# Keys, queries and values laid out in DRAM in longer runs, and fourteen staging tiles for bias rows in place of six

## The chip, the cores and the metric

The kernel runs on one core of one Trainium2 chip, in one launch. The metric is device time in microseconds (us), the median of the runs; lower is better.

## The reference

Attention with a bias that a small network makes from positions, then two feed-forward stages. Cut to what matters:

```python
# q, k, v: (2, 8, 576, 64); w1: (1, 32), b1: (32,), w2: (32, 8)
scores = scale * np.matmul(q, k.transpose(0, 1, 3, 2))
psi_rel = np.log1p(np.abs(pos[:, None] - pos[None, :]))
x = (psi_rel / psi_i)[..., None]
h = np.maximum(x @ w1 + b1, 0.0)           # 576 x 576 x 32
bias = h @ w2                              # 576 x 576 x 8, the same for both batches
scores = scores + bias.transpose(2, 0, 1)[None]
attn = softmax(scores)                     # over the last axis
x = np.matmul(attn, v)                     # then as 1152 x 512 rows
x = (silu(x @ w_gate) * (x @ w_val)) @ w_out     # 512 -> 1536 -> 512
out = softplus(x @ w_in) @ w_out2                # 512 -> 2048 -> 512
```

## The kernel before, in words

The program has three stretches. First the bias of all heads is made and laid out in SBUF, then attention runs over eight units (a pair of heads, a batch), then the two feed-forward stages follow. This change touches the first stretch and the loads of the second.

**Bias rows.** The bias is made in 36 rows of work (`order`: numbers 32 to 35 first, then 0 to 31; a row is named here by its place in this order, from 0). For a row, `hidden` (line 246) makes four hidden tiles `r` of 128 x 576 from the table `G`, three on VectorE (L260) and one on ScalarE (L258); `second` (L264) multiplies them with `w2` in sixteen small matmul passes on TensorE into a PSUM tile `pb` of which there are two; `keep` (L277) scales `pb` on ScalarE into half of a staging tile in SBUF (`early`, L280). A DMA on the queue of SyncE (SP) then takes the 128 staged partitions apart into sixteen partitions of a bias tile, eight heads of 576 each (L284; for the first four rows two DMAs of four heads each, L287). A row's staged data is 128 x 576 x 4 bytes, 288 KB. The loop makes `r` two rows ahead; there are twelve buffers for `r`, three rows.

**Staging.** `staging` (L158) walks in a circle over six halves of three tiles, which are the tags `a4`, `a5`, `a6` of the pool `xp`; `a7` holds the queries of the second unit. The tags `a0` to `a3` belong from the start to the pairs `B11` and `T1` (L121), in which the attention output and a sum are kept for the feed-forward stage; their first writer is `finish` of the first unit (L453). A staging half is written again only when the DMA out of it has landed.

**Loads.** `load` (L161) fetches a pair of heads, transposed, as 64 partitions x 2 x 576; as the tile needs the data twice, in partitions 0 to 63 and in 64 to 127, it issues two DMAs of 288 KB each, in source runs of 2304 bytes. `load_v` (L177) fetches 384 KB of values in runs of 768 bytes and two small pieces (`vt`). Issued on SP before the bias rows, after the table: keys, queries and values of the first unit, keys and queries of the second.

**What sets the order.** In the first two stretches the instructions of PE, ACT, DVE, POOL and SP stand in the order in which they are written. All DMAs of SP go round over eight semaphores, so that one is issued only when the one eight before it has landed. `run_slot` (L498) is one step of attention: scores on TensorE (L304, for the first two units), the sum with the bias on VectorE (L352), the exponential on ScalarE (L366), transposes (L401) and products with the values (L428). Four of these steps (`EARLY`, rows 23, 26, 31 and 33) run among the bias rows; the others after them. Steps are counted from 0 too: steps 0 and 1 read `bias[0]`, 2 and 3 `bias[1]`, 4 to 7 the same tiles for the second unit, 8 and 9 `bias[2]`, 10 the mixed tile, and step 11 is the first to read `bias[3]`, whose last row is the 36th.

Of the kernel before, what the change touches and what calls it, by code (L numbers as in the profile page):

```python
# [11 lines left out]
F32 = mybir.dt.float32  # L12
# [7 lines left out]
P = 128  # L20
B, H, S, D, HID = 2, 8, 576, 64, 32
NP = H // 2
# [27 lines left out]
ROWS = np.r_[:256, 512:S, 256:512]  # L50
# [47 lines left out]


@with_exitstack  # L100
def tile_kernel(ctx: ExitStack, tc, qT, kT, vS, wb, wg, wv, wo, wi, wo2, table, out):
    nc = tc.nc
    sp = nc.sync
    const = ctx.enter_context(tc.tile_pool(name="const", bufs=1))
    xp = ctx.enter_context(tc.tile_pool(name="xp", bufs=1))
# [9 lines left out]
    def slots(pool, tag, names):  # L115

        for name in names:
            n = len([1 for t in SLOTS.values() if t[0] == tag])
            SLOTS[name] = (tag, [pool.tile([P, 2, S], F32R, tag=f"{tag}{2 * n + i}", name=f"{name}{t}") for i, t in enumerate("hl")])

    slots(xp, "a", ("B11", "T1"))  # L121

    def opener(stack):
        return lambda name, bufs, **k: stack.enter_context(
            tc.tile_pool(name=name, bufs=bufs, reuse_waits="tile", **k)
        )

    rctx = ExitStack()
    with ExitStack() as actx:
# [18 lines left out]
        def new_pairs(name, count, pool=pool, **k):  # L148

            ep = pool(name, 1, **k)  # L150
            for _ in range(count):
                pairs.append(ep.tile([P, 2 * S], F32, name=f"e{len(pairs)}"))
            return ep

        new_pairs("ep0", 2)
        qraw = pool("qraw", 1)
        early = [xp.tile([P, 2, S], F32, tag=f"a{i}", name=f"early{i}") for i in range(4, 8)]
        staging = itertools.cycle([t[:, i] for t in early[:3] for i in range(2)])  # L158
        psS = pool("psS", 2, space=PSUM)

        def load(r, src, pr, b):  # L161
            for d in range(2):
                sp.dma_start(
                    out=r[D * d : D * (d + 1)], in_=src[b, 2 * pr : 2 * pr + 2].rearrange("h d s -> d h s")
                )

        def load_k(i):
            pr, b = UNITS[i]
            kr = kp.tile([P, 2, S], F32, tag="kst", name="kr") if i < PLAIN else bias[0][:, :2]
            load(kr, kT, pr, b)  # L170
            return dict(i=i, pr=pr, b=b, kr=kr)

        def load_q(u):
            u["qr"] = early[3] if u["i"] == 1 else qraw.tile([P, 2, S], F32, tag="qr", name="qr")
            load(u["qr"], qT, u["pr"], u["b"])

        def load_v(u):  # L177
            pr, b = u["pr"], u["b"]
            v = u["v"] = vp.tile([P, 4, 3 * D], F32, name="v")
            vt = u["vt"] = vts[u["i"] % 3]  # L180
            sp.dma_start(out=v, in_=vS[b, pr, :512].rearrange("(c p) e -> p c e", p=P))
            thirds = lambda ap: ap.rearrange("p (t e) -> p t e", t=3)
            sp.dma_start(out=thirds(vt[:D])[:, ::2], in_=thirds(vS[b, pr, 512:])[:, ::2])
            sp.dma_start(out=vt[D:, D : 2 * D], in_=vS[b, pr, 512:, D : 2 * D])

        def high(h, src, by="a"):
            if by == "a":
# [58 lines left out]
        def hidden(i):  # L246
            s = order[i]
            c, t = divmod(s, 8)
            rs = []
            for ct in range(4):  # L250
                if c < 4:
                    w0 = cut + GU0 - (P * c + 32 * ct + t)
                else:
                    w0 = TU0 - (P * c + 16 * ct + t)
                r = rp.tile([P, S], F32, name="r")
                n = 4 * s + ct
                if ct == 3:
                    nc.scalar.activation(r, G[:, w0 : w0 + S], AF.Relu, bias=PB[:, n : n + 1])  # L258
                else:
                    nc.vector.tensor_scalar(r, G[:, w0 : w0 + S], PB[:, n : n + 1], 0.0, op0=ALU.add, op1=ALU.max)  # L260
                rs.append(r)
            return rs

        def second(rs):  # L264
            pb = psB.tile([P, 2, 512], F32, tag="B", name="pb")
            for hf in range(2):
                for ct in range(4):
                    nc.tensor.matmul(  # L268
                        pb[32 * ct : 32 * ct + 32, hf, :HALF],
                        W2,  # L270
                        rs[ct][:, HALF * hf : HALF * (hf + 1)],
                        start=True,
                        stop=True,
                    )
            return pb

        def keep(s, pb):  # L277
            c, t = divmod(s, 8)
            st = next(staging)
            nc.scalar.activation(  # L280
                st.rearrange("p (a n) -> p a n", a=2), pb[:, :, :HALF], AF.Copy, scale=inv[:, s : s + 1]
            )
            if c < 4:
                sp.dma_start(out=bias[c][t : t + 121 : 8], in_=st)  # L284
            else:
                for a in range(2):
                    sp.dma_start(out=bias[c][D * a + t : D * a + t + 61 : 4], in_=st[a::2])  # L287
# [197 lines left out]

        units, late = [load_k(0)], []
        load_q(units[0])
        load_v(units[0])
        units.append(load_k(1))
        load_q(units[1])  # L490
        chunks = [(i, sub, n) for i in range(2 * NP) for sub in range(2) for n in range(4 + sub)]
        chunks[4:13] = chunks[9:13] + chunks[4:9]
# [76 lines left out]
        with tc.manual_schedule(engines={E.PE, E.Activation, E.DVE, E.Pool, E.SP}):  # L569
            warm = psS.tile([P, 2, 512], F32, tag="S", name="warm")  # L570
            for _ in range(WARM):
                nc.tensor.matmul(warm[:, 0, :P], ident, ident, start=True, stop=True)

            nc.vector.tensor_scalar(PB, PB, wb_sb[:, 1:2], None, op0=ALU.mult)
            nc.vector.tensor_scalar(G[:, :TW], G[:, :TW], wb_sb[:, 0:1], None, op0=ALU.mult)
            hid = [hidden(i) for i in range(2)]
            for i, s in enumerate(order):
                pb = second(hid.pop(0))
                if i == 0:
                    nc.vector.tensor_scalar(G[:, cut:], G[:, cut:], wb_sb[:, 0:1], None, op0=ALU.mult)  # L580
                if i + 2 < len(order):
                    hid.append(hidden(i + 2))
                keep(s, pb)
                if i in EARLY:
                    run_slot()
            sctx.close()
            pool = opener(actx)
            ep1 = new_pairs("ep1", 4, opener(right), side="right")
            tmpp = pool("tmpp", 1)
            t2f = tmpp.tile([P, 2, S], F32, name="t2f")  # L590
            for i, mp in enumerate((tmpp, ep1)):
                mixes.append(mp.tile([P, 5 * P], F32, name=f"m{i}"))
                nc.gpsimd.memset(mixes[-1][:, S:], 0.0)
            atp = pool("atp", 6)
            fp = pool("fp", 1)
            psT = pool("psT", 3, space=PSUM)
            psO = pool("psO", 1, space=PSUM)
            while slot < len(chunks) or jobs or turned or gathered or done or late:
                run_slot()
# [36 lines left out]
    def as_float(n):  # L636


        x = cvp.tile([P, 2 * NK, P], F32, tag="x", name="x")
        load(2 * n + 3)  # L640
        for j in range(2):
            raw, y = loaded[2 * n + j], x[:, NK * j : NK * (j + 1)]
            hw, lw, yi = raw[:, :, :, 1], raw[:, :, :, 0], y.bitcast(I32)
            if n < NL2:
                nc.scalar.activation(y, hw.bitcast(F32), AF.Prelu, scale=2.0**-112, alpha=-(2.0**32))
            else:
                nc.scalar.activation(y, hw.bitcast(F32), AF.Copy, scale=2.0**-112)  # L647
            nc.vector.tensor_scalar(yi, yi, 3, None, op0=ALU.logical_shift_left)  # L648
            if n >= NL2:
                nc.vector.scalar_tensor_tensor(yi, hw, -(2**31), yi, op0=ALU.bitwise_and, op1=ALU.bitwise_or)  # L650
            nc.vector.scalar_tensor_tensor(yi, lw, 29, yi, op0=ALU.logical_shift_right, op1=ALU.bitwise_or)  # L651
            load(2 * n + j + 4)
        return x
# [340 lines left out]
    for k in range(2):  # L994
        t4 = row()
        h, l = [ap.bitcast(F32) for ap in X["T2"][k]]
# [50 lines left out]
    with tc.manual_schedule(engines={E.PE}):  # L1047
        quads = {"z": z}
        for q in range(4):
# [5 lines left out]
            for word in f"{OTHER if q else FIRST} {TAIL}".split():  # L1055
                who, what = word
                if who in "tu":
# [7 lines left out]
                    for i, t in enumerate(TOKENS[n]):  # L1065
                        if who == "t":
                            continue
                        a, ps = acc[t // 2][:, t % 2], held[n][:, i]
# [12 lines left out]
                getattr(quads[who], "p" + what)()  # L1081


_INS = ["qT", "kT", "vS", "wb", "wg", "wv", "wo", "wi", "wo2", "table"]


# [32 lines left out]
```

## Time and profile before

| | |
|---|---|
| median of 3 runs | 596.39 us (596.32 to 596.82) |
| the profiled execution | 596.96 us |
| its span, first to last instruction | 595.0 us |
| what lies around the span | 1.96 us |
| TensorE busy over the span | 578.5 us, 97% |
| the bias rows | 5.6 us (first `r`) to 63.8 us (last staged row) |
| instructions | 11346 |

The times of the stretches below are counted from the span's start. The views used are the page, the chain of waits (what was released last, in order of time), busy time by stretch, and the timelines of single engines, which give each group of instructions with the idle time ahead of it in brackets and who ended that.

### The profile page before, as it was taken

How to read it: one execution, taken by the hardware profiler on the slowest of the kernel's cores; microseconds unless marked ns; L12 is line 12 of the kernel's file. 1: busy time of each engine (PE TensorE's matmuls, PEld its weight loads, DVE VectorE, ACT ScalarE, POOL GpSimd, SP SyncE). 2: the span in 40 equal slices, each digit the busy share in tenths (PEclk: the TensorE clock that was granted, in tenths of full speed). 3: DMA queues.
4: the chain of work that ended last, by engine and by line, in shares of the span. 5: the costliest groups of instructions: out<-in, count | busy, mean ns of one | idle time of the engine just before them, and what ended most of it. 6: DMA issues, size and time to landing. Idle time of an engine off the chain costs nothing.

```text
span 595.0 us, 11346 instructions
## 1 busy us (share of the span) xinstructions
PE 578.5 (97%) x4274; PEld 506.3 (85%) x4274; DVE 454.2 (76%) x972; ACT 375.5 (63%) x711; POOL 98.8 (17%) x147
## 2 busy tenths in 40 slices
PE   8789999999999999999999999999999999999997
PEld 5233569888887999999999999999989989988986
DVE  6799687788888999897789735679998976983432
ACT  6699877778988876665558424349735734733520
POOL 0000477778993000000000000000000000000000
PEclk9899999999999999999999999999999999999999
DMA  9999924334442333324226222222444240310012
GB/s 216 223 204 210 192 80 108 97 88 111 110 128 82 121 96 110 101 79 135 72 89 194 72 72 72 74 83 64 135 138 136 81 142 8 136 35 1 2 54 105
DMA packets 47414, 63.30 MB, mean 106 GB/s; under 512 B 4480, under 2 KB 35200, under 8 KB 47360
## 3 DMA queue, kind: packets, MB, share of 16 engines
q1 hardware_dynamic: 47216, 62.57, 38.2%
q8 instruction: 33, 0.54, 0.4%
q14 instruction: 21, 0.17, 0.1%
q10 hardware_dynamic: 144, 0.02, 0.0%
HBM read 49.60 MB, written 2.36 MB: 87 GB/s over the span
## 4 chain that ended last, share of the span: by engine, by line
PE 83%; DMA 6%; DVE 5%; ACT 3%; issue 1%; POOL 1%; SPq 0%; ACTq 0%; DVEq 0%; POOLq 0%
PE pw L726 37%; PE pw L1034 17%; PE pw L677 13%; PE po L428 6%; PE ps L331 4%; DMA bias<-early 4%; PE pt L401 3%; DMA early<-in_qT_dram 1%; PE pb L268 1%; PE ps L304 1%; DMA qr<-in_qT_dram 1%; ACT early L280 1%; DVE e L352 1%; ACT e L366 1%; DVE bias L352 0%
## 5 line engine op out<-in xcount | busy, mean ns | idle before, releaser
L1034 PE MATMUL pw<-oh,g2h 128*128 128x512 f32 x144 | 56.2, 390 | 0.0
L1034 PE MATMUL pw<-oh,g2l 128*128 128x512 f32 x144 | 56.2, 390 | 0.0
L1034 PE MATMUL pw<-ol,g2h 128*128 128x512 f32 x144 | 56.1, 390 | 0.0
L268 PE MATMUL pb<-r,wb_sb 128*32 128x288 f32 x576 | 46.6, 426 | 7.8 <-ACT early L280 6.8
L260 DVE TENSOR_SCALAR r<-G 128x576 f32<-128x576 f32 x108 | 47.7, 516 | 4.3 <-PE pb L268 4.0
L268 PEld LDWEIGHTS pb<-r,wb_sb 128*32 128x32 f32 x576 | 18.8, 112 | 34.6 <-ACT early L280 18.9
L677 PE MATMUL pw<-gl,sh 128*128 128x384 f32 x144 | 48.2, 335 | 0.0
L677 PE MATMUL pw<-gh,sl 128*128 128x384 f32 x144 | 48.2, 334 | 0.0
L677 PE MATMUL pw<-gh,sh 128*128 128x384 f32 x144 | 48.2, 334 | 0.0
L651 DVE SCALAR_TENSOR_TENSOR x<-raw,x 128x512 int32<-128x512 int32 x68 | 46.3, 688 | 0.9
L374 POOL TENSOR_SCALAR e<-e,sm 128x576 f32<-128x576 f32 x44 | 34.4, 793 | 73.2 <-DVE sm L371 66.9
L352 DVE CUSTOM_DVE_ANT_0 e<-ps,bias 128x576 f32<-128x576 f32 x44 | 33.0, 750 | 13.2 <-PE ps L331 7.6
L408 ACT COPY at<-pt 128x512 f32<-128x512 f32 (+2 forms) x69 | 36.4, 547 | 6.4 <-PE pt L401 5.9
L331 PE MATMUL ps<-kst,ql 128*128 128x288 f32 x120 | 37.0, 337 | 2.0 <-DVE sm L352 1.4
L428 PE MATMUL po<-at,v 128*64 128x256 f32 (+3 forms) x384 | 36.8, 332 | 1.0 <-DVE at L408 0.8
L1072 DVE TENSOR_TENSOR acc<-pw,acc 128x512 f32<-128x512 f32 x27 | 17.5, 686 | 25.1 <-PE pw L1034 25.1
L366 ACT ACTIVATE e<-e,sm 128x576 f32<-128x576 f32 x44 | 34.3, 780 | 2.7 <-DVE sm L352 1.7
L648 DVE TENSOR_SCALAR x<-x 128x512 int32<-128x512 int32 x68 | 28.8, 428 | 9.3 <-ACT x L647 5.1
L428 PEld LDWEIGHTS po<-at,v 128*64 128x64 f32 x384 | 26.7, 137 | 8.2 <-issue 1.3
L331 PE MATMUL ps<-kst,qh 128*128 128x288 f32 x120 | 32.1, 295 | 0.0
L1034 PEld LDWEIGHTS pw<-oh,g2l 128*128 128x128 f32 x144 | 27.0, 188 | 5.8
L401 PE MATMUL pt<-ident,e 128*128 128x128 f32 x188 | 31.6, 276 | 0.1
(269 smaller groups left out, 1657.4 us busy)
## 6 DMA issues: line engine op xcount, KB each, us to landing
raw<-in_wo_dram SPq DMA_DIRECT2D x28, 512.0 KB, 3.5
bias<-early SPq DMA_DIRECT2D x32, 288.0 KB, 7.5
raw<-in_wi_dram SPq DMA_DIRECT2D x16, 512.0 KB, 3.8
raw<-in_wv_dram SPq DMA_DIRECT2D x12, 512.0 KB, 4.5
raw<-in_wg_dram SPq DMA_DIRECT2D x12, 512.0 KB, 3.5
qr<-in_qT_dram SPq DMA_DIRECT2D x14, 288.0 KB, 4.1
bias<-in_kT_dram SPq DMA_DIRECT2D x12, 288.0 KB, 4.6
v<-in_vS_dram SPq DMA_DIRECT2D x8, 384.0 KB, 3.6
```

Of the source, the lines that this page charges most:

```text
L260: nc.vector.tensor_scalar(r, G[:, w0 : w0 + S], PB[:, n : n + 1], 0.0, op0=ALU.add, op1=ALU.max)
L268: nc.tensor.matmul(pb[32 * ct : 32 * ct + 32, hf, :HALF], W2, rs[ct][:, HALF * hf : HALF * (hf + 1)], start=True, stop=True,)
L331: nc.tensor.matmul(ps[:, hf, :HALF], u[t][:, o : o + P], kst[:, a, HALF * hf : HALF * (hf + 1)], start=i == 0, stop=i == len(parts) - 1,)
L352: nc.vector.tensor_tensor_reduce(out=e[:, :S].rearrange("p (a n) -> p a n", a=2), in0=ps[:, :, :HALF], in1=bt.rearrange("p (a n) -> p a n" ...
L366: nc.scalar.activation(e, e, AF.Exp, bias=sm[:, 0, n : n + 1], scale=-1.0, accum_out=sm[:, 1, n : n + 1])
L401: nc.tensor.transpose(pt[:, P * w : P * (w + 1)], e, ident)
L408: marks[eng, u["i"], u["sub"]] = copy(at[:, :w], pt[:, :w]).ins
L428: nc.tensor.matmul(u["po"][D * a : D * (a + 1), o : o + n], v[:, D * t : D * (t + 1)], at[:, i : i + n], start=piece == 0 and o == 0, stop ...
L651: nc.vector.scalar_tensor_tensor(yi, lw, 29, yi, op0=ALU.logical_shift_right, op1=ALU.bitwise_or)
L677: nc.tensor.matmul(ps[:, :n], w[:, k], x, start=first and k == 0 and i == 0, stop=last and k == NK - 1 and i == 2)
L726: nc.tensor.matmul(ps[:, hf, :HALF], a[:, o + k], b[:, HALF * hf : HALF * (hf + 1)], start=start and k == 0 and i == 0, stop=k == 1 and i ...
L1034: nc.tensor.matmul(ps, g, w.rearrange("p k f -> p (k f)"), start=f == 0 and i == 0, stop=f == 3 and i == 2)
```

## The change

The host lays the inputs out anew: queries and keys as 128 partitions (the 64 rows twice) of 1152 elements, a run of 4608 bytes each, and the first 512 rows of the values as 128 partitions of 768 elements, a run of 3072 bytes. The last 64 rows of the values become an input of their own, `vT`. A load of keys or queries is then one DMA of 576 KB in place of two of 288 KB; the bytes are the same. The pairs `B11` and `T1` are taken from the pool only when the bias rows are done, and the tags `a0` to `a3` serve for staging until then: fourteen halves in place of six.

```diff
-    slots(xp, "a", ("B11", "T1"))
...
-        early = [xp.tile([P, 2, S], F32, tag=f"a{i}", name=f"early{i}") for i in range(4, 8)]
-        staging = itertools.cycle([t[:, i] for t in early[:3] for i in range(2)])
+        early = [xp.tile([P, 2, S], F32, tag=f"a{i}", name=f"early{i}") for i in range(8)]
+        staging = itertools.cycle([t[:, i] for t in early[:7] for i in range(2)])
...
         def load(r, src, pr, b):
-            for d in range(2):
-                sp.dma_start(
-                    out=r[D * d : D * (d + 1)], in_=src[b, 2 * pr : 2 * pr + 2].rearrange("h d s -> d h s")
-                )
+            sp.dma_start(out=r, in_=src[b, pr].rearrange("p (h s) -> p h s", h=2))
...
-            u["qr"] = early[3] if u["i"] == 1 else qraw.tile([P, 2, S], F32, tag="qr", name="qr")
+            u["qr"] = early[7] if u["i"] == 1 else qraw.tile([P, 2, S], F32, tag="qr", name="qr")
...
-            sp.dma_start(out=v, in_=vS[b, pr, :512].rearrange("(c p) e -> p c e", p=P))
+            sp.dma_start(out=v, in_=vS[b, pr].rearrange("p (c e) -> p c e", c=4))
...
             sctx.close()
+            slots(xp, "a", ("B11", "T1"))
...
+    def twice(a):
+
+        a = a.reshape(B, NP, 2, S, D).transpose(0, 1, 4, 2, 3).reshape(B, NP, D, 2 * S)
+        return np.concatenate([a, a], 2)
+
     given = {
...
+        "qT": twice(np.stack([q[:, h][:, ROWS if h % 2 else slice(None)] for h in range(H)], 1)),
+        "kT": twice(k),
+        "vS": vs[:, :, :512].reshape(B, NP, 4, P, 3 * D).transpose(0, 1, 3, 2, 4).reshape(B, NP, P, 12 * D),
+        "vT": vs[:, :, 512:],
```

No instruction of PE, ACT, DVE or POOL changes its place. On ACT the rows that stage a bias row (the one with `early` as its output) name other tiles, and wait for other DMAs (`DMAHW` with a number is one of the eight semaphores of the DMAs). Before, the seventh row and those after it:

```order
L280 ACTIVATE early_115<-pb,G 128x576 [waits PE_49]
L258 ACTIVATE r<-G 128x576 [waits Activation_49]
L280 ACTIVATE early_113<-pb,G 128x576 [waits DMAHW7_49,DMAHW6_49,PE_49]
L258 ACTIVATE r<-G 128x576 [waits Activation_49]
L280 ACTIVATE early_113<-pb,G 128x576 [waits DMAHW1_49,DMAHW0_49,PE_49]
```

And now, from the fourteenth row:

```order
L275 ACTIVATE early_115<-pb,G 128x576 [waits PE_49]
L253 ACTIVATE r<-G 128x576 [waits Activation_49]
L275 ACTIVATE early_109<-pb,G 128x576 [waits DMAHW3_49,DMAHW2_49,PE_49]
L253 ACTIVATE r<-G 128x576 [waits Activation_49]
L275 ACTIVATE early_109<-pb,G 128x576 [waits DMAHW5_49,DMAHW4_49,PE_49]
```

The wait of row n for the DMA of row n - 6 has become one for the DMA of row n - 14. On SP the head of the queue before:

```order
L243 DMA G<-in_table_dram 128x1064
L163 DMA kr<-in_kT_dram 64x2x576 x2
L163 DMA qr<-in_qT_dram 64x2x576 x2
L181 DMA v<-in_vS_dram 128x4x192
L183 DMA vt_96<-in_vS_dram 64x2x64
L184 DMA vt_96<-in_vS_dram 64x64
L163 DMA kr<-in_kT_dram 64x2x576 x2
L163 DMA early_116<-in_qT_dram 64x2x576 x2
L287 DMA bias_89<-early_113 16x4x576 x4
```

And now:

```order
L238 DMA G<-in_table_dram 128x1064
L160 DMA kr<-in_kT_dram 128x1152
L160 DMA qr<-in_qT_dram 128x1152
L176 DMA v<-in_vS_dram 128x768
L178 DMA vt_92<-in_vT_dram 64x2x64
L179 DMA vt_92<-in_vT_dram 64x64
L160 DMA kr<-in_kT_dram 128x1152
L160 DMA early_116<-in_qT_dram 128x1152
L282 DMA bias_85<-early_109 16x4x576 x4
```

The eight DMAs of halves have become four of 128 partitions each; the order of what is loaded is the same. On ACT the first writers of `B11` and `T1` (L453 and L480) now wait for the DMAs of the rows that were last staged in those tiles, the 29th and 30th and the 33rd and 34th.

## Rows read from the trace of the kernel before

**Rows 1.** The page: busy time of the engines; DMA share in 40 slices.

```profile
PE 578.5 (97%) x4274; PEld 506.3 (85%) x4274; DVE 454.2 (76%) x972; ACT 375.5 (63%) x711; POOL 98.8 (17%) x147
DMA  9999924334442333324226222222444240310012
```

**Rows 2.** Stretches: length, busy us (instructions) of each engine, granted clock, DMA share, GB/s.

```profile
0.00:20.00 20.00, 16.30 (x152) 9.85 (x152) 15.20 (x36) 11.38 (x16) 1.29 (x9) 1.00 0.94 223
20.00:44.00 24.00, 19.49 (x252) 7.39 (x256) 19.71 (x46) 21.66 (x32) 0.00 (x0) 0.93 1.04 208
44.00:64.00 20.00, 18.88 (x228) 7.93 (x220) 17.44 (x45) 19.28 (x33) 2.27 (x3) 1.00 1.04 211
...
22.00:24.00 2.00, 1.94 (x20) 0.98 (x24) 0.00 (x0) 1.96 (x4) 0.00 (x0) 0.57 1.03 213
```

**Rows 3.** The chain that ended last: start us, us, what; DMAs from issue to landing.

```profile
10.54 8.62 DMA early<-in_qT_dram
19.17 6.79 DMA bias<-early
...
30.72 7.63 DMA bias<-early
...
41.98 7.76 DMA bias<-early
...
71.51 2.31 PE po L428 x20
```

**Rows 4.** ScalarE's timeline: start us, us, instruction, [idle before, who ended it].

```profile
11.49 0.74 ACT L280 ACTIVATE early<-pb,G 128x576 f32<-128x576 f32 x1 [0.56 <-PE pb L268]
...
15.37 0.74 ACT L280 ACTIVATE early<-pb,G 128x576 f32<-128x576 f32 x1
...
21.26 0.74 ACT L280 ACTIVATE early<-pb,G 128x576 f32<-128x576 f32 x1 [4.49 <-DMA bias<-early]
...
50.47 0.77 ACT L366 ACTIVATE e<-e,sm 128x576 f32<-128x576 f32 x1
...
63.07 0.74 ACT L280 ACTIVATE early<-pb,G 128x576 f32<-128x576 f32 x1 [0.32 <-PE pb L268]
```

**Rows 5.** VectorE's timeline, with the same columns.

```profile
8.83 11.67 DVE L260 TENSOR_SCALAR r<-G 128x576 f32<-128x576 f32 x27
24.03 1.38 DVE L260 TENSOR_SCALAR r<-G 128x576 f32<-128x576 f32 x3 [3.53 <-PE pb L268]
...
45.38 0.76 DVE L352 CUSTOM_DVE_ANT_0 e<-ps,bias 128x576 f32<-128x576 f32 x1 [0.80 <-PE ps L304]
...
51.36 0.15 DVE L370 TENSOR_SCALAR sm<-sm 128x1 f32<-128x1 f32 x1 [0.67 <-ACT e L366]
...
59.14 2.66 DVE L260 TENSOR_SCALAR r<-G 128x576 f32<-128x576 f32 x6
...
63.78 0.76 DVE L352 CUSTOM_DVE_ANT_0 e<-ps,bias 128x576 f32<-128x576 f32 x1 [1.02 <-PE ps L304]
...
74.56 0.76 DVE L352 CUSTOM_DVE_ANT_0 e<-ps,bias 128x576 f32<-128x576 f32 x1 [2.51 <-PE ps L304]
```

**Rows 6.** TensorE's timeline: one bias row.

```profile
33.50 1.18 PE L268 MATMUL pb<-r,wb_sb 128*32 128x288 f32 x16 [0.28 <-ACT early L280]
```

**Rows 7.** L284, its last DMA (duration ns, first to last issue us; landing).

```profile
L284 SPq DMA_DIRECT2D bias<-early x1: 532/532/532, 63.8 to 63.8; - x1
...
DMA to landing us min/median/max: 6.9/6.9/6.9
```

**Rows 8.** L163, the first half of the second unit's keys.

```profile
L163 SPq DMA_DIRECT2D kr<-in_kT_dram x1: 595/595/595, 7.1 to 7.1; - x1
...
DMA to landing us min/median/max: 8.0/8.0/8.0
```

**Rows 9.** L628, the first three weight loads, 512 KB over 128 partitions each.

```profile
L628 SPq DMA_DIRECT2D raw<-in_wv_dram x2: 373/440/507, 173.0 to 174.0; - x2
...
DMA to landing us min/median/max: 3.7/4.7/5.6
```

More of the change, by code (lines that the diff above doesn't have):

```diff
@@ L100, in tile_kernel @@
 @with_exitstack
-def tile_kernel(ctx: ExitStack, tc, qT, kT, vS, wb, wg, wv, wo, wi, wo2, table, out):
+def tile_kernel(ctx: ExitStack, tc, qT, kT, vS, vT, wb, wg, wv, wo, wi, wo2, table, out):
     nc = tc.nc
@@ L180, in load_v @@
             vt = u["vt"] = vts[u["i"] % 3]
-            sp.dma_start(out=v, in_=vS[b, pr, :512].rearrange("(c p) e -> p c e", p=P))
+            sp.dma_start(out=v, in_=vS[b, pr].rearrange("p (c e) -> p c e", c=4))
             thirds = lambda ap: ap.rearrange("p (t e) -> p t e", t=3)
-            sp.dma_start(out=thirds(vt[:D])[:, ::2], in_=thirds(vS[b, pr, 512:])[:, ::2])
-            sp.dma_start(out=vt[D:, D : 2 * D], in_=vS[b, pr, 512:, D : 2 * D])
+            sp.dma_start(out=thirds(vt[:D])[:, ::2], in_=thirds(vT[b, pr])[:, ::2])
+            sp.dma_start(out=vt[D:, D : 2 * D], in_=vT[b, pr, :, D : 2 * D])
         def high(h, src, by="a"):
@@ L1081, in tile_kernel @@
                 getattr(quads[who], "p" + what)()
-_INS = ["qT", "kT", "vS", "wb", "wg", "wv", "wo", "wi", "wo2", "table"]
+_INS = ["qT", "kT", "vS", "vT", "wb", "wg", "wv", "wo", "wi", "wo2", "table"]
 def kernel(q, k, v, w1, b1, w2, moe_w_gate, moe_w_val, moe_w_out, moe2_w_in, moe2_w_out):
@@ L1095 @@
         small[rows, 0], small[rows, 1], small[rows, 2 + 8 * g : 10 + 8 * g] = w1[0], b1, w2
+    vs = np.concatenate([v[:, ::2], np.roll(v[:, 1::2], -D, 2), v[:, 1::2]], 3)
+    def twice(a):
+        a = a.reshape(B, NP, 2, S, D).transpose(0, 1, 4, 2, 3).reshape(B, NP, D, 2 * S)
+        return np.concatenate([a, a], 2)
     given = {
-        "qT": np.stack([q[:, h][:, ROWS if h % 2 else slice(None)] for h in range(H)], 1).transpose(0, 1, 3, 2),
-        "kT": k.transpose(0, 1, 3, 2),
-        "vS": np.concatenate([v[:, ::2], np.roll(v[:, 1::2], -D, 2), v[:, 1::2]], 3),
+        "qT": twice(np.stack([q[:, h][:, ROWS if h % 2 else slice(None)] for h in range(H)], 1)),
+        "kT": twice(k),
+        "vS": vs[:, :, :512].reshape(B, NP, 4, P, 3 * D).transpose(0, 1, 3, 2, 4).reshape(B, NP, P, 12 * D),
+        "vT": vs[:, :, 512:],
         "wb": small,
```

## The prediction

> **What bounds the kernel now.** I read the page first. TensorE is busy for 97% of the span, so time can only be won where it waits, and the DMA engines are at 9 tenths or more in the first five slices alone, some 74 us [rows 1]. The table by stretch narrows this: from 20 to 64 us the DMA share is 1.04, no engine of the sixteen is ever empty, at about 210 GB/s, while DVE is busy for 37.2 of these 44 us and ACT for 40.9 [rows 2]. The chain of waits says who holds whom: from 10.5 to 50 us it goes from DMA to DMA, each 7 to 9 us from issue to landing, with short ScalarE steps between [rows 3]. ScalarE's timeline has the place: unstalled it stages a row each 1.29 us (11.49 to 15.37 is three rows), then it waits 4.49 us for the first bias DMA to give a staging half back [rows 4]. From there on the row's pace is the DMA's: the issues at 30.72 and 41.98 stand eight rows apart, 1.41 us a row [rows 3]. [...]
>
> **How late the DMA may be.** After the rows the work is attention's own. The last bias DMA is issued at 63.84 and lands 6.9 us later, at 70.7 [rows 7]; its first reader, step 11, starts at 74.56 on VectorE and had waited for TensorE [rows 5], which was at products until 73.8 [rows 3]. So the bias data is 3.8 us ahead of its need at the end, though it holds the rows back at the start. What counts for the end is when step 4 can start: 63.78 now, after the last `r` ends at 59.14 + 2.66 = 61.8 and TensorE's last rows behind it [rows 5].
>
> **Fourteen staging halves.** The wait for the DMA of row n - 6 becomes one for row n - 14. In its new place row 14 (counted from 0) is staged by ScalarE at 11.49 + 12 x 1.29 = 27 us and needs row 0, whose two DMAs landed before 21.3 when staging went on [rows 4]; the backlog grows by 1.41 - 1.29 = 0.12 us a row, 2.5 us by row 35, so the wait does not come back. Who is late next:
> VectorE. From 8.83 it makes 27 tiles in 11.67 us, 0.432 us each [rows 5]. Up to the end of the last `r` it has 102 of them, 44.1 us; three sums of the early steps at 0.76, 2.3; and two small operations, 0.3. That ends at 8.83 + 46.7 = 55.5, where it now ends at 61.8: a gain of 6.3. Two waits in this stretch are not for a DMA: 0.80 for scores and 0.67 for an exponential [rows 5]. If both stay, the gain is 4.8. Most of them should go, since they arise while VectorE runs up to two rows ahead of a held ScalarE; at its own pace it arrives later. I keep a third, 0.5: 5.8.
> ScalarE. Rows 2 to 35 at 1.29, and three exponentials at 0.77: the last row would be staged at 11.49 + 42.7 + 2.3 = 56.5 against 63.07 [rows 4], a gain of 6.6: close, but VectorE is the bound.
> TensorE. A row takes 1.18 us [rows 6] and gives 0.11 us of room against 1.29; its idle stretch and the low clock behind it go too.
> So step 4 starts 5.8 us sooner, at 58.0, and step 11 at 68.8 if the bias is there.
>
> **The loads.** Eight halves and the values stand in the queue ahead of the rows. The first half of the second keys lands at 7.1 + 8.0 = 15.1 [rows 8] and the last half of the queries, three later, at 10.54 + 8.62 = 19.2 [rows 3]: 1.35 us for 288 KB. Weight loads over 128 partitions land two in (174.0 + 5.6) - (173.0 + 3.7) = 2.9 us, 1.45 us for 512 KB [rows 9], so 576 KB cost 1.63 in place of 2.70. Four of these pairs: 4.3 us. The values, 384 KB in one DMA over 128 partitions before and after, I cost at no gain; were they as slow as a half now, and as fast as the weights then, it would be 1.80 - 1.09 = 0.7 us. So the bias DMAs, which queue behind, start 4.3 us sooner and keep their 1.41 (the queue was full and stays full), and the last row lands at 70.7 - 4.3 = 66.4, 2.4 us before step 11 wants it. Bounds of this term: 0 (loads as slow as now) to 5.0. Its worth for the end by itself is nothing; it keeps the last row off the path, which at 70.7 would hold step 11 up by 1.9. The later loads, two DMAs fewer a unit on SP, lie under TensorE's work: the chain from 71 us on is compute [rows 3], and I cost them at nothing. The second unit's values and the third unit's keys queue behind the last bias row in the same order as now, and land 4.3 us sooner or, if loads gain nothing, when they do now.
>
> [...]
>
> **B11 and T1.** Their first writers on ScalarE now wait for rows staged late. T1 waits for the 34th of the 36, which is to land two rows ahead of the last, at 66.4 - 2.8 = 63.6; B11 for the 30th, about 57.9. `finish` of the first unit comes after the products that end at 73.8 now [rows 3], so at 68.0: B11's wait is 10 us over by then, and T1 comes later still. Queued behind it on ScalarE would be copies for the products; I cost it at nothing.
>
> **The rivals.**
> 1. The loads stay as slow as they are, and the last row ends the matter. The run lengths are what the change names, and the weights' loads speak against run length as the cause: theirs are of 1024 bytes, shorter than the 2304 now, and are faster. Then only the joining of halves could help, and if it doesn't, the last row lands at 70.7, step 11 starts there and not at 74.56: a gain of 3.8, 592.6. [...]
> 2. The three engines don't reach their own pace together: the two waits stay, and the other three early steps too cost VectorE the 0.8 that the first does now. The gain is 4.8 - 2.4 = 2.4, 594.0. For it: the coupling is tight, two PSUM tiles, three rows of `r`. Against: only the first sum shows such a wait.
> 3. Eight DMAs in flight slow each other. In rows: 36 rows take 70.7 - 19.2 = 51.5 us now, 1.43 each. From 19.2 - 4.3 = 14.9 they would take the last past 68.8 at a pace over 1.50, and so eat into the gain; at 1.66 step 11 is no sooner than now, and at 1.70, a fifth slower, the last lands at 76.1, 1.5 past 74.56: 597.9, slower than before. Against it: the share is 1.04 already, so each engine has always had a next packet; for it, only that six in flight is all the trace shows.
> 4. The gain is real and is lost again, in attention or at the start of the feed-forward stage: 596.4. The chain has no DMA after 50 us that is not a wait of compute, so I find no place for it.
>
> **How the numbers follow.** The profiled execution has a span of 595.0 and a time of 596.96; 5.8 off makes 589.2 and 591.2. Against the median, 0.57 lower, it is 596.39 - 5.8 = 590.6. Chances: the forecast (gain 4.8 to 6.6) 0.70; rival 1, 0.12; rival 2, 0.06; rival 4, 0.06; rival 3, 0.03; some gain past 6.6, out of waits in attention that I hold for compute, 0.03. The range goes from 589.4 (a gain of 7.0) to 593.2 (rival 1 with some of rival 2, 3.2). What can be told from no change is about 0.2%, 1.2 us. Faster: 0.70 + 0.12 + 0.06 + 0.03 = 0.91; slower: rival 3, 0.03; the same: 0.06.
>
> **What would show it.** Right: no wait of ScalarE for `bias<-early` in its timeline; VectorE's last `r` ends near 56; TensorE's clock stays at 1.00 from 22 to 26; DMA still full to 66; step 11 near 69 with TensorE, not a DMA, ahead of it. Wrong: a wait for `bias<-early` ahead of step 11 (rival 1 or 3), four waits for scores among the rows (rival 2), or a chain through loads in attention (rival 4).

## The result, and the profile after

The changed kernel takes 589.62 us (median of 4 runs, 589.42 to 590.08) against 596.36 for the kernel before in the runs beside it: a ratio of 0.9891, with a 95% interval of 0.9873 to 0.9908. The profiled execution takes 589.42 us with a span of 587.6, so 7.5 us less than the one before; between the medians it is 6.7.

The rows of the kernel after, in the order of those of before. The page: busy time of the engines, and the DMA share in 40 slices.

```profile
PE 579.3 (99%) x4274; PEld 509.9 (87%) x4274; DVE 452.9 (77%) x972; ACT 374.1 (64%) x711; POOL 98.9 (17%) x147
DMA  8999623333233342232344231222343241310012
```

The DMA engines are at nine tenths or more in three slices where it was five [rows 1]. By stretch (length, busy us of each engine, granted clock, DMA share, GB/s):

```profile
0.00:20.00 20.00, 18.44 (x187) 11.80 (x188) 15.53 (x36) 14.94 (x22) 1.30 (x9) 1.00 0.91 288
20.00:44.00 24.00, 24.00 (x294) 11.02 (x292) 24.00 (x58) 23.66 (x37) 0.00 (x0) 1.00 1.04 205
44.00:64.00 20.00, 19.21 (x194) 9.16 (x186) 17.95 (x53) 18.86 (x38) 6.53 (x10) 1.00 1.05 211
22.00:24.00 2.00, 2.00 (x28) 0.96 (x22) 2.00 (x6) 2.00 (x4) 0.00 (x0) 1.00 1.05 215
```

From 20 to 44 us TensorE and VectorE are busy without a gap and ScalarE all but, where VectorE had 19.7 and ScalarE 21.7 us [rows 2]; the granted clock is 1.00 from 22 to 24 us where it was 0.57 [rows 2], and the DMA, at the same 1.04 and 205 GB/s, no longer holds anyone. The ends of matmuls are modelled in this profile, so its 24.00 us of TensorE don't tell whether TensorE or VectorE sets the pace now; the last experiment does. VectorE's timeline (start us, us, instruction, idle time ahead of it and who ended that) says it in five lines:

```profile
4.43 0.30 DVE L569 TENSOR_SCALAR G<-G,wb_sb 128x144 f32<-128x144 f32 x1 [4.43 <-DMA wb_sb<-in_wb_dram]
8.49 31.02 DVE L255 TENSOR_SCALAR r<-G 128x576 f32<-128x576 f32 x72
52.41 2.65 DVE L255 TENSOR_SCALAR r<-G 128x576 f32<-128x576 f32 x6
57.02 0.76 DVE L347 CUSTOM_DVE_ANT_0 e<-ps,bias 128x576 f32<-128x576 f32 x1 [1.00 <-PE ps L299]
67.82 0.76 DVE L347 CUSTOM_DVE_ANT_0 e<-ps,bias 128x576 f32<-128x576 f32 x1 [2.51 <-PE ps L299]
```

72 hidden tiles stand in one piece of 31.02 us, 0.431 each, where 27 stood before the first gap [rows 5]. The last ends at 55.06 (61.80 before), step 4 starts at 57.02 (63.78), and step 11 at 67.82 (74.56), still with TensorE ahead of it. ScalarE has no wait for `bias<-early` left:

```profile
11.15 0.74 ACT L275 ACTIVATE early<-pb,G 128x576 f32<-128x576 f32 x1 [0.35 <-PE pb L263]
56.33 0.74 ACT L275 ACTIVATE early<-pb,G 128x576 f32<-128x576 f32 x1 [0.31 <-PE pb L263]
```

One thing must be taken off before terms are compared. VectorE starts when the first DMA lands, at 4.43 here, at 4.77 in the profile of before, and between 4.42 and 5.12 in the kernels below, without regard to the change. Counted from its own first instruction, step 4 comes 59.0 us later before and 52.6 after: the bias rows gained 6.4 us, and the other 0.34 is the start.

The loads on SP: the second unit's keys and queries, and the last bias row (duration ns, first to last issue us; landing).

```profile
L160 SPq DMA_DIRECT2D kr<-in_kT_dram x1: 622/622/622, 4.5 to 4.5; - x1
L160 SPq DMA_DIRECT2D early<-in_qT_dram x1: 430/430/430, 5.2 to 5.2; - x1
...
DMA to landing us min/median/max: 6.7/7.3/7.9
```

```profile
L279 SPq DMA_DIRECT2D bias<-early x1: 1073/1073/1073, 57.1 to 57.1; - x1
...
DMA to landing us min/median/max: 7.3/7.3/7.3
```

The queries are there at 13.1 where it was 19.2 [rows 3], and the last bias row lands at 64.4 where it was 70.7 [rows 7]. The chain of waits goes through one bias DMA in place of the string of them [rows 3], and then through TensorE:

```profile
31.34 5.95 DMA bias<-early
37.28 1.63 DVE r L255 x4
41.38 2.66 DVE r L255 x6
46.72 3.73 PE pb L263 x43
```

VectorE has no idle time there (its 72 tiles run past 39 us), so this DMA is a link of the chain that held nobody.

### The profile page after: what moved, and what is told of

The parts are those of the page before. It is cut to its first block, busy times and chain, and to the rows that moved or that the text cites. A ratio compares the mean times of both kernels' runs of the same rounds, so it can differ in the third digit from the quotient of the medians.

```text
span 587.6 us, 11306 instructions
## 1 busy us (share of the span) xinstructions
PE 579.3 (99%) x4274; PEld 509.9 (87%) x4274; DVE 452.9 (77%) x972; ACT 374.1 (64%) x711; POOL 98.9 (17%) x147
## 4 chain that ended last, share of the span: by engine, by line
PE 85%; DVE 7%; ACT 4%; POOL 2%; DMA 1%; issue 1%; POOLq 0%; DVEq 0%; ACTq 0%
PE pw L722 38%; PE pw L1030 17%; PE pw L673 13%; PE po L423 6%; PE ps L326 4%; PE pt L396 3%; PE pb L263 2%; ACT early L275 2%; ACT r L253 2%; DVE e L347 2%; PE ps L299 1%; DVE r L255 1%; DMA bias<-early 1%; PE warm L567 1%; DVE bias L347 1%
## 5 line engine op out<-in xcount | busy, mean ns | idle before, releaser
L369 POOL TENSOR_SCALAR e<-e,sm 128x576 f32<-128x576 f32 x44 | 34.5, 795 | 66.3 <-DVE sm L366 58.9
L263 PEld LDWEIGHTS pb<-r,wb_sb 128*32 128x32 f32 x576 | 21.6, 109 | 24.4 <-DVE r L255 9.0
```

What stands on the lines that cost most here:

```text
L263: nc.tensor.matmul(pb[32 * ct : 32 * ct + 32, hf, :HALF], W2, rs[ct][:, HALF * hf : HALF * (hf + 1)], start=True, stop=True,)
L369: nc.gpsimd.tensor_scalar(e, e, sm[:, 3, i : i + 1], 1.0, op0=ALU.mult, op1=ALU.mult)
```

## The experiments

All were timed beside the kernel before, in three groups (596.64, 595.45 and 595.82 us for it; 596.36 beside the changed kernel). As it differs by 1.2 us between groups, some tenths between kernels of different groups say little in the medians; where the text goes by them, it goes by the traces. The table has what the traces say of each; step 4 is counted from VectorE's first instruction.

| kernel | last query load lands | last bias row lands | step 4 | us, median | ratio to before |
|---|---|---|---|---|---|
| before | 19.2 | 70.7 | 59.0 | 596.36 | |
| after | 13.1 | 64.4 | 52.6 | 589.62 | 0.9891 [0.9873, 0.9908] |
| staging only | 17.8 | 68.4 | 52.7 | 592.83 | 0.9942 [0.9922, 0.9961] |
| layout only | 13.2 | 64.6 | 52.7 | 590.65 | 0.9904 [0.9889, 0.9919] |
| 128 partitions, 2304 B | 14.1 | 65.6 | 52.6 | 590.31 | 0.9896 [0.9878, 0.9913] |
| halves, 4608 B | 18.3 | 68.8 | 52.6 | 593.03 | 0.9945 [0.9928, 0.9962] |
| rows alternate | 13.2 | 61.5 | 52.6 | 589.55 | 0.9903 [0.9889, 0.9918] |
| GpSimd helps | 13.2 | 73.1 | 64.8 | 601.85 | 1.0109 [1.0094, 1.0124] |
| both of these | 14.5 | 73.3 | 64.9 | 601.88 | 1.0109 [1.0088, 1.0130] |
| four halves | 13.5 | 65.1 | 55.3 | 593.24 | 0.9964 [0.9951, 0.9977] |
| fewer tiles | 13.8 | 64.9 | 48.9 | 586.90 | 0.9851 [0.9837, 0.9866] |
| fewer tiles, rows alternate | 13.5 | 58.9 | 48.9 | 586.77 | 0.9850 [0.9829, 0.9870] |
| six halves, late pairs | 13.0 | 65.2 | 52.6 | 589.87 | 0.9903 [0.9886, 0.9919] |

### Each part by itself

The changed kernel with the old loads and the old layout in DRAM (the values' loads and the host's part, also as before, are not shown):

```diff
-            sp.dma_start(out=r, in_=src[b, pr].rearrange("p (h s) -> p h s", h=2))
+            for d in range(2):
+                sp.dma_start(
+                    out=r[D * d : D * (d + 1)], in_=src[b, 2 * pr : 2 * pr + 2].rearrange("h d s -> d h s")
+                )
```

> Fourteen staging halves, loads as before (two DMAs of 64 partitions a pair, runs of 2304 bytes). Theory A, staging frees the engines and the loads only keep the last bias row off the path: step 4 of attention starts near 57 to 58 us as in the changed kernel, the last bias row still lands near 70.5, step 11 waits for it and starts there in place of 67.8; 592.4 us, a gain of 4.0 where the whole change gave 6.7. Theory B, the gain comes from the loads and six halves were enough: no gain, 596.4. If step 11 doesn't wait for the last row, both have the bias wrong.

The changed kernel with the new loads and the old six staging halves:

```diff
+    slots(xp, "a", ("B11", "T1"))
...
-        early = [xp.tile([P, 2, S], F32, tag=f"a{i}", name=f"early{i}") for i in range(8)]
-        staging = itertools.cycle([t[:, i] for t in early[:7] for i in range(2)])
+        early = [xp.tile([P, 2, S], F32, tag=f"a{i}", name=f"early{i}") for i in range(4, 8)]
+        staging = itertools.cycle([t[:, i] for t in early[:3] for i in range(2)])
...
-            slots(xp, "a", ("B11", "T1"))
```

> New loads, six staging halves as before. The prediction's own account (loads are worth nothing by themselves, row n is still held by row n - 6 at the DMA's 1.41 us a row): the last row is staged near 61 to 62 us, a gain of 1 to 2, 594.5 to 595.5. Theory B, worked out from the changed kernel's landings: the first row lands at 13.6, before row 6 wants its half at 16.3, so the 4.5 us wait goes without more staging; row n - 6 lands at about 6.1 + 1.41 n, where the engines want it at 8.6 + 1.29 n, so it holds them from about row 21 on, and the last row is staged within 1 us of 56.3: a gain of 5.7 to 6.7, 589.6 to 590.7.

Staging alone gives 3.8 us and the layout alone 6.0, against 6.7 for both: they overlap, and the layout does nearly all of it. The ratios of the layout alone and of both have intervals that overlap, so what the staging adds to it isn't told from nothing here. With staging only, step 4 is as early as after, so the rows are as quick; the gain is given back where the DMAs are late. VectorE at steps 11 to 14 of that kernel, and two pieces of its chain:

```profile
68.73 0.76 DVE L350 CUSTOM_DVE_ANT_0 e<-ps,bias 128x576 f32<-128x576 f32 x1 [3.06 <-PE pt L399]
69.45 0.76 DVE L350 CUSTOM_DVE_ANT_0 e<-ps,bias 128x576 f32<-128x576 f32 x1
71.04 0.75 DVE L350 CUSTOM_DVE_ANT_0 e<-ps,bias 128x576 f32<-128x576 f32 x1
74.30 0.75 DVE L350 CUSTOM_DVE_ANT_0 e<-ps,bias 128x576 f32<-128x576 f32 x1
```

```profile
53.71 10.60 DMA bias<-early
64.32 8.91 DMA bias<-in_kT_dram
```

The idle time ahead of step 11 names TensorE, yet the last row lands at 68.37 and the next sum follows after 0.72 us where it was 1.27 after: the step waited for the row, 0.6 us, and the next sum makes up all of it but 0.1. The dearer hold is the second one, which the prediction didn't price. The third unit's keys wait behind the rows in SP's queue, land at 64.32 + 8.91 = 73.2, and step 14 starts at 74.30 where it was at 72.67 after. Counted from VectorE's first instruction that is 1.4 us later, and of the gain of 6.3 us at step 10, 5.0 is left. The traced execution took 591.93 us; the 0.9 us that the median has on top of it stand in no trace.

With the layout only, ScalarE's timeline lists no idle time for a staging half, and step 4 is 0.1 later than after. Six halves are enough (how nearly, the section on the depth tells) once the first bias DMA lands at 13.7 us in place of 20.6.

### Run length or the joining of halves

One DMA of 128 partitions from runs of 2304 bytes:

```diff
-            sp.dma_start(out=r, in_=src[b, pr].rearrange("p (h s) -> p h s", h=2))
+            sp.dma_start(out=r, in_=src[b, 2 * pr : 2 * pr + 2].rearrange("h p s -> p h s"))
...
-        a = a.reshape(B, NP, 2, S, D).transpose(0, 1, 4, 2, 3).reshape(B, NP, D, 2 * S)
+        a = a.transpose(0, 1, 3, 2)
```

> The changed kernel, but keys and queries in one DMA of 128 partitions with runs of 2304 bytes as before. If the joining of the halves is what made the loads faster (theory of the prediction), a load lands 1.4 to 1.7 us after the one before it, the last queries at 13 to 14 us, time 589.6. If run length did it, the pair costs 2.5 to 2.7, the last queries land near 18, the last bias row near 69 to 70, and the time is 591.5 to 592.5.

Two DMAs of 64 partitions from runs of 4608 bytes:

```diff
-            sp.dma_start(out=r, in_=src[b, pr].rearrange("p (h s) -> p h s", h=2))
+            for d in range(2):
+                rows = slice(D * d, D * (d + 1))
+                sp.dma_start(out=r[rows], in_=src[b, pr, rows].rearrange("p (h s) -> p h s", h=2))
```

> The changed kernel, but each load of keys or queries as two DMAs of 64 partitions, with runs of 4608 bytes. If the halves are what is slow: 2.5 to 2.7 us a pair as in the kernel before, last queries near 17.5 to 18.5, last bias row near 69, time 591 to 592. If run length did it: 1.4 to 1.6 a pair, 589.6.

The last load of queries, joined with short runs, and the last half of it with long ones:

```profile
L160 SPq DMA_DIRECT2D early<-in_qT_dram x1: 468/468/468, 5.6 to 5.6; - x1
...
DMA to landing us min/median/max: 7.0/7.8/8.6
```

```profile
L162 SPq DMA_DIRECT2D early<-in_qT_dram x1: 465/465/465, 10.4 to 10.4; - x1
...
DMA to landing us min/median/max: 7.8/7.8/7.8
```

They land at 14.1 (the first view has two loads, and 8.6 is the queries' way) and 18.3. From the landing of the table's first piece, which is the first DMA to land on SP, it is 8.8 us to there in the changed kernel and 9.2 with short runs joined, against 13.3 with staging only (halves, short runs), 13.8 with halves in long runs, and 14.6 in the kernel before. The first unit's joined loads land 1.47 to 1.52 us after the DMA ahead of them in short runs, and 1.42 to 1.44 in the changed kernel. The times follow: 590.31 goes with the layout's 590.65, and 593.03 with the 592.83 of staging alone, with the same second hold in its chain (the traced execution lies below the median here too, at 591.88). The joining is the effect; the run length named in the change brings at most 0.1 us a joined load, and with halves nothing that shows.

### How deep the staging must be

Four halves; and six, with `B11` and `T1` taken from the pool late as in the changed kernel:

```diff
-        staging = itertools.cycle([t[:, i] for t in early[:7] for i in range(2)])
+        staging = itertools.cycle([t[:, i] for t in early[:2] for i in range(2)])
```

```diff
-        staging = itertools.cycle([t[:, i] for t in early[:7] for i in range(2)])
+        staging = itertools.cycle([t[:, i] for t in early[:3] for i in range(2)])
```

> The changed kernel with four staging halves. A row's DMA takes 4.4 to 4.9 us from issue to landing when the queue is short, plus 0.74 to stage: four rows in 5.2 to 5.7 us, 1.30 to 1.43 a row. Theory: the depth has to cover this time and no more; with four the wait is back, the last row is staged 3 to 6 us later than 56.3, time 592.5 to 595.5. Rival: four are enough too, as six nearly are, and the time is within 1.5 of 590.6.

> The new layout, with the pairs B11 and T1 taken from the pool late as in the changed kernel, but six staging halves. To tell what the 0.8 us between the layout alone (590.65) and the whole change (589.6 to 589.85) is. Theory: of it 0.2 us is the depth itself (step 4 at 57.2 against 57.0) and 0.6 us is the phase of VectorE against GpSimd at steps 44 to 50, where either one or the other's instruction is stretched; this kernel then comes out at either 589.8 or 590.6, by the phase, with step 4 at 57.2. Rival: the depth has a cost of its own in attention; then it is 590.6 with a wait that names a staging tile, B11 or T1.

With four, ScalarE's waits are back, in the middle of the rows (in the third of these lines the idle time names TensorE, but the row that it needs landed 0.09 us ahead):

```profile
24.37 0.74 ACT L275 ACTIVATE early<-pb,G 128x576 f32<-128x576 f32 x1 [0.47 <-DMA bias<-early]
25.94 0.74 ACT L275 ACTIVATE early<-pb,G 128x576 f32<-128x576 f32 x1 [0.16 <-DMA bias<-early]
27.98 0.74 ACT L275 ACTIVATE early<-pb,G 128x576 f32<-128x576 f32 x1 [0.63 <-PE pb L263]
```

and step 4 is 2.7 us later. With six the timeline lists no such wait, step 4 is where it is with fourteen, and the time is 589.87, not told apart from 589.62. The wait is there all the same, in pieces too short to be listed as idle time: rows 19 to 26 are all staged 0.08 to 0.11 us behind the landing of the row six ahead. Row 23 with six halves, and in the changed kernel:

```profile
39.03 0.75 ACT L275 ACTIVATE early<-pb,G 128x576 f32<-128x576 f32 x1
```

```profile
38.25 0.82 ACT L275 ACTIVATE early<-pb,G 128x576 f32<-128x576 f32 x1
```

Counted from VectorE's first instruction it is 0.6 us late. From row 27 on, among the early steps, the row that is needed has landed 0.4 us or more ahead, and row 29 is on time again. So six just do, and the eight further halves bring nothing measurable beside the new loads.

This leaves the layout alone, at 590.65, some 0.8 us behind a kernel of another group (0.6 in the traces; the ratios to before are the same, 0.9904 and 0.9903) that differs from it only in when `B11` and `T1` are taken, and so in which tags are staged in. The place is one step in attention. VectorE in the layout alone, then in the kernel with six halves and late pairs, and then GpSimd in that one:

```profile
129.20 1.12 DVE L445 TENSOR_TENSOR bias<-bias,B11l 128x320 f32<-128x320 f32 x1
```

```profile
129.23 0.55 DVE L443 TENSOR_TENSOR bias<-bias,B11l 128x320 f32<-128x320 f32 x1
129.25 1.07 POOL L369 TENSOR_SCALAR m<-m,sm 128x576 f32<-128x576 f32 x1
```

In all thirteen traces these two instructions start within 35 ns of each other, and one of them is stretched: VectorE's to 1.1 us in three kernels (GpSimd's then takes 0.74 to 0.77), GpSimd's to 1.05 to 1.1 in the other ten. The three are the layout alone, 128 partitions with 2304 B, and fewer tiles; the last two have fourteen halves and late pairs, so neither the six halves nor the early pairs decide it. Where it is VectorE's, step 45 is 0.6 us late and stays late. VectorE's record starts first in all thirteen, so the order of the starts doesn't tell which of the two is stretched; what does was not shown.

### The order of the rows

```diff
-        order = [32, 33, 34, 35, *range(32)]
+        order = [32, 33, 34, 35, *(8 * c + t for c in range(4) for t in (0, 4, 1, 5, 2, 6, 3, 7))]
```

> The changed kernel, but the eight rows of a bias tile in the order 0 4 1 5 2 6 3 7 (same work, each row to the same sixteen partitions). Theory: the row's DMA pace is set by which partitions a row and its neighbours in the queue write; 1.41 to 1.53 while neighbours lie next to each other, 1.25 to 1.3 where the row number goes from 3 to 4, every fourth landing now. Then the pace falls to 1.25 to 1.30 and the last row lands at 58 to 61 in place of 64.4. Rival: the pace is the bytes' own, 1.43 again. For the time both say the same, 589.6 within 0.8, if the engines and not the DMAs set the rows' pace in the changed kernel; a gain over 1 us would show that the DMA still does.

```profile
20.00:44.00 24.00, 24.00 (x292) 11.11 (x292) 24.00 (x58) 23.66 (x37) 0.00 (x0) 1.00 0.98 231
44.00:64.00 20.00, 19.21 (x196) 9.33 (x190) 17.96 (x52) 18.89 (x38) 6.46 (x10) 1.00 0.74 209
```

In these windows of the kernel with alternate rows the DMA share falls to 0.98 and 0.74, with 231 GB/s in the first: between 28 and 37 us the rows land 1.24 to 1.27 us apart, where it is 1.30 to 1.53 in the changed kernel. After that the queue runs short of rows, and landings follow the staging. The last row lands at 61.5 in place of 64.4, half a microsecond past the range expected, and the time is the same. So the DMA does not set the end any more. Why the rows land closer together in this order was not shown; each goes to the same sixteen partitions as before, and only its neighbours in the queue are others.

### GpSimd for some of the tiles

In every second row GpSimd makes one hidden tile, in turn one of VectorE's and ScalarE's:

```diff
-                if ct == 3:
+                if (i % 4, ct) in ((1, 2), (3, 3)):
+                    nc.gpsimd.tensor_scalar(r, G[:, w0 : w0 + S], PB[:, n : n + 1], 0.0, op0=ALU.add, op1=ALU.max)
+                elif ct == 3:
```

> The changed kernel, but GpSimd makes one hidden tile in every second row, in turn one of VectorE's and one of ScalarE's. Theory: VectorE (1.30 us a row) and ScalarE (1.29) set the pace together; they go to 1.19 and 1.13, TensorE with 1.18 to 1.23 becomes the bound, and step 4 starts 1.5 to 2.5 us sooner; of that at most 3.4 can be had before the last bias row (64.4) holds step 11. 587.2 to 588.2. Rival: GpSimd and VectorE hold each other up while both read SBUF, an r on GpSimd takes well over 0.8 us, and step 4 starts no sooner or later: 589.6 or more.

The same, with the alternate order of rows:

> Both of the last two: if each does what its theory says, 587.0 to 588.0 with the last bias row well ahead of step 11; if GpSimd's help costs, as e6_pool_helps.

Both are slower than before. The hidden tiles by engine (ns least, median, most; first and last start):

```profile
L253 POOL TENSOR_SCALAR r<-G x18: 2426/2642/3018, 5.4 to 64.4; 128x576 f32<-128x576 f32 x18
```

```profile
L257 DVE TENSOR_SCALAR r<-G x99: 499/508/1007, 5.3 to 66.3; 128x576 f32<-128x576 f32 x99
```

A GpSimd tile takes 2.6 us beside VectorE (its scaling of 128 x 576 took 0.75 above), and VectorE's reach 1.0: 34 of its 99 take over 0.56 us, where 1 of 108 does in the changed kernel. The order of the rows changes nothing in it: again not the DMA.

### What sets the pace now

The changed kernel without these same tiles, the row's second tile standing in for them, in both orders of rows:

```diff
+                if (i % 4, ct) in ((1, 2), (3, 3)):
+                    rs.append(rs[1])
+                    continue
                 r = rp.tile([P, S], F32, name="r")
```

> The changed kernel with a part of the work left out: in every second row one hidden tile is not made, and the second hidden tile of the row is used in its place (VectorE's third tile in one row of four, ScalarE's in another of four), so the output is not the reference's; TensorE and the DMAs keep all their work. Theory: VectorE (and ScalarE beside it) sets the pace of the bias rows now, 1.29 us a row, and TensorE has 0.11 us of room in each (1.18). Then VectorE saves 9 x 0.431 = 3.9 us, TensorE allows 34 x 0.11 = 3.7, step 4 starts near 53.3 in place of 57.0; the DMA keeps 1.43 a row, its last row lands near 64.4 and is now the one that is late, by some 0.3 to 0.6 us, for a step 11 that would want it at 64.1: 586.3. Rival: TensorE itself needs 1.29 in an unbroken row of rows; then step 4 stays at 57.0 and the time at 589.6. Rival: the DMA still binds; then nothing changes either and ScalarE waits for bias<-early again.

> As the kernel with fewer hidden tiles (the same tiles left out, so the output is not the reference's), with the rows of a tile in the order 0 4 1 5 2 6 3 7, in which the DMA was quicker. Theory: step 4 near 53.3 and the last row landing by 61, so that nothing holds step 11: 585.8 to 586.0, and the difference to the kernel in the old order, 0.3 to 0.6 us, is what the DMA would cost there. Rival, TensorE sets the pace: 589.6 for both.

```profile
8.73 28.45 DVE L258 TENSOR_SCALAR r<-G 128x576 f32<-128x576 f32 x66
65.14 0.76 DVE L350 CUSTOM_DVE_ANT_0 e<-ps,bias 128x576 f32<-128x576 f32 x1 [2.83 <-DMA v<-in_vS_dram]
```

Step 4 comes 3.7 us sooner, counted from the start, as expected; the DMA, at an unchanged 1.43 us a row, is then the late one: the last row lands at 64.9 and step 11 starts at 65.1, 0.3 us late, which the next sum, 0.95 us behind in place of 1.27, makes up again (the idle time names the values' DMA, which this sum doesn't read; the row landed 0.2 us ahead of it). With the alternate order, whose last row is there at 58.9, step 11 has TensorE ahead of it again:

```profile
64.53 0.76 DVE L350 CUSTOM_DVE_ANT_0 e<-ps,bias 128x576 f32<-128x576 f32 x1 [2.51 <-PE ps L302]
```

The two medians, 586.90 and 586.77, are not told apart; the hold is read from the timeline alone. The first kernel also has VectorE's side stretched at step 45. VectorE and ScalarE set the pace of the rows in the changed kernel, and the DMA has some 3 us left before it holds step 11 again.

## Why the prediction was right

The forecast was 590.6, the time is 589.62, in its range, by the mechanism that it named: VectorE's own pace became the bound of the rows. The two spans differ by 7.4 us: 0.3 is the start, 6.4 the bias rows, 0.7 attention, put down to the later loads below; the medians differ by 6.7. The sum had 5.8, so it was short by the 0.5 kept for two waits, by 0.1 of pace and by the 0.7 in attention. The gain lies 0.1 past the 4.8 to 6.6 that had a chance of 0.70, in the case with 0.03, and something in attention is what that case names. By its steps:

- **VectorE as the next bound** held to 0.1 us: 6.3 forecast, 6.4 measured from the start. The 0.5 us kept for the two waits on scores and exponential was a mis-sized term: VectorE's timeline shows no idle time between 8.49 and the last `r`, so it should have been 0. Coupling between the three engines, rival 2, doesn't show.
- **The loads** were mis-sized on the safe side, though not by the pairs. From landing to landing the four pairs take 9.7 us before, 2.4 each where the sum had 2.70 from the last three halves alone, and 5.9 after, 1.47 each where it had 1.63, since the weights' row [rows 9] was the nearest there was: 3.8 saved, 4.3 forecast. That the last queries land 6.1 us sooner is for the rest the table's second piece, ahead of them and the same in both kernels, which lands 1.3 us behind the first in place of 2.5, the values (costed at no gain with up to 0.7 as the bound), 1.25 against 1.84, smaller pieces 0.2, and the start 0.3. The values' own layout is not what shortens them: they take 1.39 in the old one with staging only, and 1.88 in the new one beside halves; why is open. The last row lands at 64.4 where 66.4 was forecast. The pace of the rows stayed as forecast: 1.43 against 1.40.
- **"Its worth for the end by itself is nothing"** is the step that failed. The layout alone gives 6.0 of the 6.7 us. The prediction followed the wait of row 6 into the staging and never asked what six halves would do if the queue ahead of them were 6 us shorter: the first wait, 4.49 us [rows 4], was a wait for eight loads to leave the queue and not for bias rows. The backlog that is left after it, 0.14 us a row, lengthens the way from the start of staging to landing from 6.1 us at row 0 to 7.7 at row 13 (kernel with six halves), which is just what six halves allow, 6 x 1.29; so they hold rows 19 to 26 alone, by 0.6 us at most. The forecast of the sum didn't suffer, since both parts were in the change.
- **Rival 1** (loads stay slow) is the kernel with staging only: 592.83 measured against 592.6. That the sum is right is luck, since its parts are not: the last row was 2.3 us sooner than the rival had it, the hold at step 11 was made up by the next sum, and the third unit's keys, which the prediction costs at nothing, held step 14 by 1.4 us.
- **Rivals 3 and 4** fall: the rows keep their pace with more in flight, and nothing is lost later.
- **The later loads, at nothing**, hide 0.7 us. From step 11 to the first product of the feed-forward stage it is 120.97 us before and 120.30 after, and the difference appears between steps 49 and 52. VectorE there before:

```profile
144.25 0.96 DVE L190 CAST kst<-bias 128x576 fp32r<-128x576 f32 x1 [0.27 <-issue]
...
146.24 1.14 DVE L194 TENSOR_TENSOR kst<-bias,kst 64x288 fp32r<-64x288 f32 x1
```

And after:

```profile
137.08 0.45 DVE L185 CAST kst<-bias 128x576 fp32r<-128x576 f32 x1
...
139.00 0.46 DVE L189 TENSOR_TENSOR kst<-bias,kst 64x288 fp32r<-64x288 f32 x1 [0.47 <-ACT kst L183]
```

These are the copies of a unit's keys. The first stands 0.27 us idle before, on nothing that the profile shows; on this line VectorE's queue has 12 waiting instructions before and 4 after, and one load in place of two is one DMA fewer to wait for. Steps 49 to 50 take 2.50 us in all three kernels whose loads come in halves (before, staging only, halves of 4608) and 1.64 in all ten others. Before, the two copies start 0.11 and 0.02 us after a GpSimd instruction (at 144.14 and 146.22) and take 0.96 and 1.14; after, the first starts 0.61 us after one (at 136.47, 0.75 us long) and takes 0.45, and the second 0.11 us ahead of one (at 139.11) and takes 0.46. That the added wait is what brings this about was not tried by itself.

## What to carry to other kernels

When a wait for a buffer is first seen, ask what its transfer stands behind in the queue before adding buffers: here the new loads gave nearly the whole gain, and eight more staging halves nothing that can be measured beside them: the kernel with six halves ties with the changed one, and no kernel here that does the whole work beats it by more than the noise. A wait can hold an engine without being listed as idle time: compare each start with the landing that it needs. Price the parts of a change both alone and together, and follow each queue past the last transfer that you think of, since the next loads in it can be the ones that hold. Before comparing instants of two profiles, take off the difference in when their first DMA landed.

## What the runs showed of the hardware that was not expected

- Loads in halves of 64 partitions bring the last queries 13.3 to 14.6 us after the table's first piece, loads of 128 partitions in 8.6 to 9.2 (10.3 in one kernel of ten), whether the runs in DRAM are 2304 or 4608 bytes.
- The pace of DMAs into sixteen partitions each differed with which partitions the neighbours in the queue write: 1.43 us a row in order, and 1.24 to 1.27 in the alternate order from 28 to 37 us; with fewer tiles to make, at a full share of 1.05, it was 1.21 to 1.27 in that same order from 28 to 43 us.
- Which of two instructions on VectorE and GpSimd that start within 35 ns is stretched moved the end by 0.6 us, so kernels that differ in nothing near that place can differ by 0.1% for it.
